# Second MoE's input weights scaled per item and made while they are narrowed, next block's differences spread over steps, and the tail's maxima in three steps

## The chip, the cores and the metric

One Trainium2 chip, one core of it. The metric is the device time of one execution in microseconds, median of several runs. TensorE (PE) multiplies, VectorE (DVE), ScalarE (ACT) and GpSimd (POOL) do the elementwise work, SyncE (SP) issues nearly all transfers.

## The reference, cut to what matters

```python
# q, k, v: (4, 8, 576, 64); rotary embedding on q and k, softmax attention, then
x = attn_out.transpose(0, 2, 1, 3).reshape(2304, 512)
h = np.maximum(np.maximum(x @ w1, x @ w2), x @ w3)      # 512 x 768 each
y = h @ w_out1                                          # 768 x 512
h = y @ w_in                                            # moe2_w_in: 512 x 2048
g = h * (1.0 / (1.0 + np.exp(-h)))
out = g @ w_out                                         # moe2_w_out: 2048 x 512
```

The weights arrive as 64-bit floats.

## The kernel before, in words

The program has three stages on one core: attention with the first MoE woven in, a tail in which the last batch's first MoE runs alone, and the second MoE.

**Attention.** Four batches of 4 head pairs and 5 query tiles make 80 tile steps (0 to 79), 20 a batch. A step issues its scores on PE (`tile_scores`), their row maximum on DVE (`tile_max`, L453, tile `nb`), two exponentials on ACT (L460), and for older tiles the normalisation (L472), the moves of the probabilities over DMA (`tile_move`, L511, `pt<-e`, four transfers a step on SP's queue), the flip of what they brought on DVE (`tile_flip`, L533) and the products with v (`av`, L578). Between them groups of the first MoE (`group`, L673) are put out by a budget written out by hand (`pace`, `RATE`), so the order of the work on PE is fixed when the program is built; a scheduler that is part of the build may move other engines' instructions within what `issue_after` allows.

**Narrowing.** The 64-bit weights of the second MoE are turned into 32-bit ones by `narrow_w2`, in pieces of 128x256: 32 pieces of `wi` (the input weights), then 32 of `wo`. A piece is loaded (L858), cast on ACT (L229), gets its low bits on DVE in three instructions (L241, L248, L249) and is measured on ACT (L155, a sum of squares into a column of `W.mx`). Each is then stored to DRAM (`zwi`, `zwo`). From step 20 the generator `wprep3` is advanced once a step and once more at every fourth: 1.25 pieces a step. After the 32nd piece the columns are turned into a bound (`root`, three small DVE instructions, L160 to L162, and a reduce, L263), and its maximum over partitions is found: `all_max_a` turns the column on PE (L122) and reduces the row on DVE (L124), `all_max_b` spreads it back over partitions on PE (L130), and `scale_of` makes a power-of-two scale and its inverse in four small DVE instructions (L145 to L148).

**Items.** With `wi`'s one scale known, `prep_w8` makes 16 items, one each 1.7 steps: it loads 128x512 of `zwi` back (`za`), forms four sums or differences of 128x128 blocks on POOL (L971, `zs`), and casts each half to a high (ACT, L948) and a low (DVE, L952) 16-bit part (`w8o`), which go to DRAM (`w8scr`, L979). The second MoE reads them from there.

**The tail.** When attention is done, `for n, _ in enumerate(moe)` runs the last batch's first MoE. At n = 9 `y_split` takes the first block's maximum (L165), turns it, spreads it and casts the block; at n = 15 the same is done for the next (`y7_max`, `y_scales`).

**The second MoE.** The first block goes through `s1`, then four passes J = 0..3, each over two blocks with 8 steps p. `s1_pair` makes 42 products per step with combinations of blocks (a fast product scheme with seven forms); its results are added up on DVE (L1109) and POOL (L1117) and go through a Silu on ACT (L1121). `g_split` makes four sums on POOL (L1050, `gsum`) and casts (L1054, L1055); `second` multiplies with `wo` (L1166). For the next J the block is loaded at p = 0, its maximum taken at p = 1, and at p = 2 `y7_sums` makes its scale and its four differences of 128x512 on POOL (L1138, the list `DIFFS`). The forms follow from p = 3 on.

Of the kernel before, what the change touches and what calls it, by code (L numbers as in the profile page):

```python
# [17 lines left out]
P = 128  # L18
# [4 lines left out]
def fused_kernel(  # L23
# [67 lines left out]
    z_p = right("z_p", 4)  # L91
# [18 lines left out]
    zscr = {nm: dram.tile([P, KC * (F2 // 512) * 512], F32, name="z" + nm) for nm in ("wi", "wo")}  # L110
# [72 lines left out]
    class Weights:  # L183
# [76 lines left out]
        def row_max(self, lo=0, n=None, ma=None):  # L260
            ma = ma or self.maxima(lo, n or self.m)
# [7 lines left out]

        def scale_a(self, n):  # L270
            return all_max_a(self.row_max(0, n))
# [548 lines left out]
    def narrow_w2(W, src, nm):  # L820

        part = {}
        M = W.m * 512 // 256
        for n in range(M + 5):
            if n >= 5:
                W.measure(n - 5)
                if nm == "wi":
                    i, o = divmod(n - 5, 2)  # L830
                    q, c = divmod(i, KC)
                    half, f = divmod(4 * q + 2 * o, HB)
                    nc.sync.dma_start(
                        out=zscr[nm].rearrange("p (f c a i n) -> p f c a i n", c=2, a=2, i=2, n=P)[:, f:f + 2, c % 2, c // 2, half],
                        in_=W.t[n - 5].rearrange("p (f n) -> p f n", n=P),
                    )
                else:
                    nc.sync.dma_start(out=zscr[nm][:, (n - 5) * 256:(n - 4) * 256], in_=W.t[n - 5])
            if 3 <= n <= M + 2:
                with tc.issue_after(last["max"]):  # L840
                    W.narrow_low(part.get(n - 3))
                    W.narrow_b(n - 3, part.pop(n - 3, None))
            if 2 <= n <= M + 1:
                if wide:
                    W.t[n - 2] = z_p.tile([P, 256], F32, tag="z", name="z")
                with tc.issue_after(exps[-1]):
                    W.narrow_a(n - 2, part.get(n - 2), low=False)
            if n < M:
                i, o = divmod(n * 256, 512)
                if nm == "wi":  # L850
                    q, c = divmod(i, KC)
                    from_ = src[c * P:(c + 1) * P, q * 512 + o:q * 512 + o + 256]
                else:
                    from_ = src[i * P:(i + 1) * P, o:o + 256]
                if wide:
                    part[n] = z64_p.tile([P, 256], w1.dtype, tag="z64", name="z64")
                    with tc.issue_after(last["load"]):
                        nc.sync.dma_start(out=part[n], in_=from_)  # L858
                else:
                    W.t[n] = z_p.tile([P, 256], F32, tag="z", name="z")  # L860
                    nc.sync.dma_start(out=W.t[n], in_=from_)
            yield
        t = W.scale_a(n=M)
        yield
        with tc.issue_after(last["score"]):
            W.scale_b("s" + nm, t)
        yield
# [14 lines left out]
    def y_scales(m, w, st):  # L882

        s, i = scale_of(all_max(m), 1, "y")
# [4 lines left out]
        ch = small.tile([P, 1], F32, tag="ch", name="ch")  # L889
        nc.vector.tensor_scalar(out=ch, in0=co, scalar1=2.0 * w, scalar2=None, op0=ALU.mult)  # L890
# [6 lines left out]
    def y_split(r, pool, st):  # L897
        r = flat(r[:, 0:2])
        m = small.tile([P, 1], F32, tag="ym", name="ym")
        absmax(m, r)  # L900
        s, sg, ch, co = y_scales(m, 1, st)
# [21 lines left out]
    SUMS = ((4, 0, 2, ALU.add), (6, 1, 0, ALU.subtract), (5, 4, 1, ALU.subtract), (7, 3, 5, ALU.subtract))  # L923
    DIFFS = ((4, 0, 1), (6, 2, 0), (5, 2, 4), (7, 3, 5))

    HB = NF2 // 2
# [26 lines left out]

    def prep_w8(step):

        sw = half_of(WI, "wi")
        steps = []

        def item(k):
            f, c = divmod(k, 2)  # L960
            z, w = {}, {}

            def load():
                z[0] = za_p.tile([P, 4, P], F32, tag="za", name="za")
                nc.sync.dma_start(out=flat(z[0]), in_=zscr["wi"][:, (2 * f + c) * 512:(2 * f + c + 1) * 512])

            def sums():
                z[4] = zs_p.tile([P, 4, P], F32, tag="zs", name="zs")
                block = lambda i: z[i // 4 * 4][:, i % 4]
                for o, x, y, op in SUMS:  # L970
                    nc.gpsimd.tensor_tensor(out=block(o), in0=block(x), in1=block(y), op=op)  # L971

            def high(a):
                w[a] = w8o_p[0].tile([P, 2, 4, P], F16, tag="w8o", name="w8o")
                cast_high(flat(w[a][:, 0]), flat(z[a]), sw, exps[-1])

            def low(a):
                cast_low(flat(w[a][:, 1]), flat(w[a][:, 0]), flat(z[a]), sw, last["max"])
                nc.sync.dma_start(out=w8scr[:, f, c, :, a:a + 4], in_=w[a])  # L979

# [465 lines left out]
```

## Time and profile before

| | |
|---|---|
| median of 3 runs | 968.85 us (968.54 to 969.66) |
| profiled execution, whole | 970.68 us |
| its span, first to last instruction | 969.0 us |
| granted clock, mean | 0.983 |
| PE busy | 901.6 us (93%) |
| DVE, ACT, POOL busy | 709.6, 609.4, 441.1 us |
| moved by DMA | 146.29 MB |

Busy time is what the profiler records of an engine's own instructions. Matmuls are pipelined, so a busy PE can still be slower than its best. Attention ends near 550 us, the tail near 624 us.

### The profile page before, as it was taken

To read this page: it belongs to the slowest core of one execution; us is meant where nothing else is said; L and a number is where in the kernel's file an instruction comes from. 1 tells how busy PE (TensorE), PEld (TensorE's weight loads), DVE (VectorE), ACT (ScalarE), POOL (GpSimd) and SP (SyncE) were. 2 spreads that over 40 slices of the span, in tenths; PEclk is the share of its full clock that TensorE was granted. 3 is DMA by queue.
4 is the path that set the end of the run, shared out by engine and by line. 5 is a ranking of instruction groups with operands and counts; after the bars stand their busy time and mean duration, and the time that the engine had idled before them with its cause. 6 is when DMAs were issued, how large, how long until landed. Compare 5 with 4: busy or idle time off the path is not lost.

```text
span 969.0 us, 19018 instructions
## 1 busy us (share of the span) xinstructions
PE 901.6 (93%) x6802; PEld 669.0 (69%) x6802; DVE 709.6 (73%) x1271; ACT 609.4 (63%) x1405; POOL 441.1 (46%) x482
## 2 busy tenths in 40 slices
PE   3887998999999999989998999999998999999997
PEld 1443665666665666656654687788887888888886
DVE  6779888877788676898887677465786766856654
ACT  1987677757788777789877534363654545545442
POOL 6745485870325502321211047264486467464363
PEclk9799998999999999999999999999999999999999
DMA  6953035858888985899999763273543434424101
GB/s 154 285 146 108 14 100 126 186 110 179 200 172 196 221 159 135 218 241 228 263 223 204 183 206 110 63 230 113 157 158 99 136 122 136 127 87 137 61 1 44
DMA packets 178798, 146.29 MB, mean 151 GB/s; under 512 B 50960, under 2 KB 160272, under 8 KB 178704
## 3 DMA queue, kind: packets, MB, share of 16 engines
q1 hardware_dynamic: 177200, 144.36, 58.0%
q8 instruction: 54, 0.88, 0.4%
q10 hardware_dynamic: 1504, 0.72, 0.3%
q14 instruction: 40, 0.33, 0.1%
HBM read 90.51 MB, written 26.21 MB: 120 GB/s over the span
## 4 chain that ended last, share of the span: by engine, by line
PE 54%; DMA 8%; DVE 8%; ACT 5%; POOL 4%; issue 3%; SPq 3%; DVEq 0%; ACTq 0%; POOLq 0%
PE m L673 12%; PE m L1103 7%; DMA pt<-e 5%; PE mb L1103 5%; PE c L1166 4%; PE b L1166 4%; PE a L1166 3%; PE xp L578 3%; PE s L443 3%; PE mg L673 3%; POOL gsum L1050 2%; PE d L1166 2%; SPq L511 2%; DVE pt L533 1%; DVE nb L453 1%
## 5 line engine op out<-in xcount | busy, mean ns | idle before, releaser
L673 PEld LDWEIGHTS <-w 128*128 128x128 f16 x1632 | 159.1, 98 | 61.0 <-issue 17.8
L673 PE MATMUL m<-x,w 128*128 128x256 f16 (+1 forms) x1356 | 186.9, 286 | 10.6 <-DVE t L692 5.4
L1166 PEld LDWEIGHTS <-g 128*128 128x128 f16 x1485 | 145.8, 98 | 17.2
L1103 PEld LDWEIGHTS <-w8s 128*128 128x128 f16 x1344 | 131.2, 98 | 16.3 <-issue 1.0
L453 DVE TENSOR_REDUCE nb<-s 128x2 f32<-128x1152 f32 (+1 forms) x80 | 98.6, 1233 | 40.7 <-PE s L443 34.1
L460 ACT ACTIVATE e<-s,nb 128x576 f32<-128x576 f32 x144 | 105.3, 736 | 29.8 <-DVE nb L453 27.2
L472 ACT ACTIVATE e<-e,rec 128x576 f32<-128x576 f32 x144 | 104.1, 767 | 9.3 <-DVE rec L470 8.9
L366 POOL TENSOR_TENSOR w<-qk,sin_sb 128x512 f32<-128x512 f32 (+2 forms) x40 | 43.4, 1087 | 128.1 <-DMA qk<-in_q_dram 122.5
L443 PE MATMUL s<-T 64*128 64x512 f32 x256 | 80.7, 701 | 0.0
L578 PE MATMUL xp<-pt,vd 128*64 128x256 f32 (+1 forms) x512 | 76.5, 414 | 0.2 <-DVE pt L533 0.2
L533 DVE STREAM_TRANSPOSE pt<-pt 128x1024 f32<-128x1024 f32 (+1 forms) x60 | 67.7, 1129 | 11.9 <-DMA pt<-e 11.6
L971 POOL TENSOR_TENSOR zs<-za 128x128 f32<-128x128 f32 x32 | 17.1, 554 | 119.9 <-DVE w8o L952 46.1
L1117 POOL TENSOR_TENSOR z<-t 128x256 f32<-128x256 f32 x32 | 27.1, 847 | 89.0 <-DVE t L1109 53.9
L1055 DVE SCALAR_TENSOR_TENSOR g<-gsum,sg,g 128x1024 f16<-128x1024 f32 x36 | 49.2, 1372 | 24.5 <-ACT g L1054 24.1
L1054 ACT ACTIVATE g<-gsum,sg 128x1024 f16<-128x1024 f32 x36 | 40.9, 1143 | 37.8 <-POOL gsum L1050 37.8
L673 PE MATMUL m<-h,wo 128*128 128x256 f16 (+1 forms) x448 | 61.7, 286 | 0.0
L673 PEld LDWEIGHTS <-wo 128*128 128x128 f16 x512 | 49.7, 98 | 14.7 <-issue 2.0
L578 PEld LDWEIGHTS xp<-pt,vd 128*64 128x64 f32 x512 | 35.1, 136 | 34.4 <-issue 12.3
L944 POOL TENSOR_TENSOR z<-z 128x256 f32<-128x256 f32 x32 | 30.1, 964 | 42.1 <-DMA z<-zwo 41.6
L1166 PE MATMUL b<-w,g 128*128 128x256 f16 x376 | 48.5, 273 | 0.0
L1166 PE MATMUL c<-w,g 128*128 128x256 f16 x376 | 48.1, 274 | 0.0
L1166 PE MATMUL a<-w,g 128*128 128x256 f16 x376 | 47.9, 273 | 0.0
(266 smaller groups left out, 1998.1 us busy)
## 6 DMA issues: line engine op xcount, KB each, us to landing
w8s<-w8scr SPq DMA_DIRECT2D x64, 448.0 KB, 4.3
pt<-e SPq DMA_DIRECT2D x192, 128.0 KB, 4.1
z<-in_moe_w_in_dram SPq DMA_DIRECT2D x32, 256.0 KB, 3.6
z<-in_moe_w_out_dram SPq DMA_DIRECT2D x32, 256.0 KB, 3.9
w8scr<-w8o SPq DMA_DIRECT2D x32, 256.0 KB, 3.6
w<-in_moe_w_dram SPq DMA_DIRECT2D x6, 768.0 KB, 5.0
wo<-in_moe_w_dram SPq DMA_DIRECT2D x6, 768.0 KB, 5.4
qk<-in_q_dram SPq DMA_DIRECT2D x32, 128.0 KB, 3.6
```

Of the source, the lines that this page charges most:

```text
L366: tt(out=w4, in0=t4, in1=sin2, op=ALU.mult)
L443: last["s"] = last["score"] = nc.tensor.matmul(s[:, o:o + 512], qs[r], kt[r], start=True, stop=True).ins
L453: x = nc.vector.tensor_reduce(out=nb[:, 0:m], in_=both(s, 0, 960, 576) if m > 1 else s[:, 0:576], op=ALU.max, axis=AX.X, negate=True)
L460: x = nc.scalar.activation(out=e[:, HK[g]], in_=s[:, SK[g]], func=AF.Exp, bias=nb[:, g:g + 1], accum_out=sm[:, g:g + 1])
L472: nc.scalar.activation(out=e[:, HK[g]], in_=e[:, HK[g]], func=AF.Copy, scale=r[:, g:g + 1])
L533: nc.vector.transpose(out=x, in_=x)
L578: nc.tensor.matmul(xp[r, 0:n], v4[:, g, c, :], turned(c, g), start=False, stop=(c == 3))
L673: x = nc.tensor.matmul(ps[:, 0:n], l, r, start=(first and i == 0), stop=(not more and i == len(passes) - 1))
L1054: nc.scalar.activation(out=h, in_=x, func=AF.Copy, scale=sg_t[jb])
L1055: nc.vector.scalar_tensor_tensor(out=l, in0=x, scalar=sg_t[jb], in1=h, op0=ALU.mult, op1=ALU.subtract)
L1103: nc.tensor.matmul(o, l, r, start=(i == 0), stop=(i == len(passes) - 1))
L1166: x = nc.tensor.matmul(ps, l, r, start=first, stop=last_, skip_group_check=True)
```

## The change

- `narrow_w2` handles `wi` and `wo` in one run of 70 iterations. A piece is placed straight into a half of a `za` tile (two pieces are one item's four blocks); the ring `za` grows from 2 to 4 tiles, the ring `z` goes. The pieces of `wi` are loaded in the items' order, as two rows of 1 KB per partition and not one of 2 KB.
- Each pair of items (f = 0..7) has a scale of its own, from its four pieces: taken, turned and spread in three iterations (`scale_m`, `scale_a`, `scale_b`). Items are then made at once: sums in iterations 4f + 8 and 4f + 9, highs from 4f + 9 to 4f + 12, lows from 4f + 10 to 4f + 13. `zwi` and its loads and stores go, `prep_w8` goes.
- `wi`'s overall scale and `wo`'s are still found, each in three iterations. `wo`'s narrowed pieces are stored two at a time.
- `ch` becomes a tile of 8 columns, one for each f, and the Silu in `s1` is split in two halves, each with its own column.
- The four differences of the next J are issued one a step, at p = 1 to 4.
- In the tail the maximum is taken at n = 8, turned at n = 9, spread at n = 10 (and 15, 16, 17 for the next block), the PE part behind the last group.

```diff
-            if hasattr(WI, "s"):
-                wprep4 = wprep4 or prep_w8(1.7)
-                next(wprep4, None)
+            za_p.bufs = 4
             for _ in range(1 + (j % 4 == 0) if j > 20 else 0):
                 next(wprep3, None)
...
+    def wi_scale(f, m):
+        e = rare.tile([P, 1], F32, tag="wie", name="wie")
+        ei, hi, ii = e.bitcast(I32), half_wi.bitcast(I32)[:, f:f + 1], inv_wi.bitcast(I32)[:, f:f + 1]
+        nc.vector.tensor_scalar(out=e, in0=m, scalar1=2.0 ** -45, scalar2=None, op0=ALU.max)
+        nc.vector.tensor_scalar(out=ei, in0=ei, scalar1=EXPMASK, scalar2=None, op0=ALU.bitwise_and)
+        nc.vector.tensor_scalar(out=hi, in0=ei, scalar1=-1, scalar2=266 << 23, op0=ALU.mult, op1=ALU.add)
+        nc.vector.tensor_scalar(out=ii, in0=ei, scalar1=13 << 23, scalar2=None, op0=ALU.subtract)
+
+    def narrow_w2(WI, WO):
...
+        def load(n):
+            W, i = which(n)
+            if W is WI:
+                k, a = divmod(i, 2)
+                f, c = divmod(k, 2)
+                from_ = wi2[(2 * a + c) * P:(2 * a + c + 1) * P, :].rearrange("p (i f n) -> p f i n", i=2, n=P)[:, f]
...
+        def sums(k):
+            zs[k] = zs_p.tile([P, 4, P], F32, tag="zs", name="zs")
+            block = lambda i: (z, zs)[i // 4][k][:, i % 4]
+            for o, x, y, op in SUMS:
+                nc.gpsimd.tensor_tensor(out=block(o), in0=block(x), in1=block(y), op=op)
...
+        def low(k, a):
+            t = w.pop((k, a))
+            f, c = divmod(k, 2)
+            cast_low(flat(t[:, 1]), flat(t[:, 0]), flat((z, zs)[a][k]), half_wi[:, f:f + 1], last["max"])
+            nc.sync.dma_start(out=w8scr[:, f, c, :, 4 * a:4 * a + 4], in_=t)
+
+        def scale_m(f):
+            m = ma[f] = rare.tile([P, 1], F32, tag="wim", name="wim")
+            nc.vector.tensor_reduce(out=m, in_=WI.maxima(4 * f, 4), op=ALU.max, axis=AX.X)
+
+        def scale_a(f):
+            with tc.issue_after(last["score"]):
+                ma[f] = all_max_a(ma[f])
+
+        def scale_b(f):
+            with tc.issue_after(last["score"]):
+                m = all_max_b(ma.pop(f))
+            wi_scale(f, m)
...
+        for n in range(2 * M + 6):
+            for f in range(HB):
+                if 7 <= n - 4 * f <= 9:
+                    (scale_m, scale_a, scale_b)[n - 4 * f - 7](f)
+            scale_all(n, WI, M + 5, "swi")
+            scale_all(n, WO, 2 * M + 3, "swo")
...
-        ch = small.tile([P, 1], F32, tag="ch", name="ch")
-        nc.vector.tensor_scalar(out=ch, in0=co, scalar1=2.0 * w, scalar2=None, op0=ALU.mult)
+        ch = small.tile([P, HB], F32, tag="ch", name="ch")
+        nc.vector.tensor_scalar(out=ch, in0=inv_wi, scalar1=i, scalar2=2.0 * w, op0=ALU.mult, op1=ALU.mult)
...
-                nc.scalar.activation(
-                    out=g[:, 2 * half:2 * half + 2].rearrange("p t (i n) -> p i t n", i=2),
-                    in_=ps.rearrange("p (i t n) -> p i t n", i=2, t=2), func=AF.Silu, scale=ch,
-                )
+                for e in range(2):
+                    nc.scalar.activation(
+                        out=g[:, 2 * half:2 * half + 2, e * P:e * P + P],
+                        in_=ps[:, e * 256:e * 256 + 256].rearrange("p (t n) -> p t n", t=2), func=AF.Silu, scale=ch[:, 2 * u + e:2 * u + e + 1],
+                    )
...
+        def y7_diffs(J, r, diffs):
             with tc.issue_after(last["gsum"]) if J else nullcontext():
-                for o, x, y in DIFFS:
+                for o, x, y in diffs:
                     nc.gpsimd.tensor_tensor(out=y7_block(r, o), in0=y7_block(r, x), in1=y7_block(r, y), op=ALU.subtract)
...
                 if p == 1 and more:
                     m = y7_max(raw)
+                    raw = y7_place(J + 1, raw)
+                if 0 < p < 5 and more:
+                    y7_diffs(J + 1, raw, DIFFS[p - 1:p])
...
-        if n == 9:
-            st["y0"] = y_split(y0, yt_p, st)
+        with tc.issue_after(last["group"]):
+            if n in (9, 16):
+                top = all_max_a(top)
+            if n in (10, 17):
+                top = all_max_b(top)
+        if n == 8:
+            top = small.tile([P, 1], F32, tag="ym", name="ym")
+            absmax(top, flat(y0[:, 0:2]))
+        if n == 10:
+            st["y0"] = y_split(y0, top, yt_p, st)
...
         if n == 15:
-            st["y7s"] = y_scales(y7_max(st["y7"]), 2, st)
+            top = y7_max(st["y7"])
+        if n == 17:
+            st["y7s"] = y_scales(top, 2, st, True)
```

## Rows read from the trace of the kernel before

**Rows 1.** Page, busy us of each engine, share of the span, instructions.

```profile
PE 901.6 (93%) x6802; PEld 669.0 (69%) x6802; DVE 709.6 (73%) x1271; ACT 609.4 (63%) x1405; POOL 441.1 (46%) x482
```

**Rows 2.** Busy time by stretch: stretch and its length, then each engine, clock, DMA.

```profile
192.00:230.00 38.00, 36.67 (x249) 23.74 (x248) 30.41 (x50) 24.81 (x71) 19.51 (x20) 1.00 0.68 142
230.00:385.00 155.00, 150.71 (x1018) 97.14 (x1017) 117.27 (x230) 117.07 (x332) 44.47 (x47) 1.00 0.83 177
385.00:545.00 160.00, 148.53 (x990) 94.18 (x989) 134.48 (x266) 132.36 (x366) 35.05 (x63) 1.00 0.95 227
583.00:675.00 92.00, 92.00 (x783) 76.39 (x783) 52.64 (x74) 44.89 (x67) 45.34 (x47) 1.00 0.41 131
732.00:750.00 18.00, 15.26 (x123) 12.49 (x122) 10.33 (x26) 8.05 (x12) 10.84 (x10) 0.91 0.36 109
```

**Rows 3.** DVE timeline: the maxima that open steps 30 and 55.

```profile
230.15 0.76 DVE L453 TENSOR_REDUCE nb<-s 128x1 f32<-128x576 f32 x1 [0.76 <-PE s L434]
...
384.93 1.36 DVE L453 TENSOR_REDUCE nb<-s 128x2 f32<-128x1152 f32 x1 [1.89 <-PE s L443]
```

**Rows 4.** Tile z by stretch: DVE, ACT and POOL busy with its instructions.

```profile
230.00:385.00 155.00, 28.60 (x72) 22.11 (x72) 0.00 (x0) 1.00 0.83 177
385.00:545.00 160.00, 32.74 (x93) 28.09 (x92) 0.00 (x0) 1.00 0.95 227
```

**Rows 5.** Tile w8o by stretch: DVE and ACT busy with its instructions.

```profile
230.00:385.00 155.00, 0.75 (x1) 1.33 (x2) 1.00 0.83 177
385.00:545.00 160.00, 24.87 (x31) 21.05 (x30) 1.00 0.95 227
```

**Rows 6.** Groups of DVE instructions, 150 to 560 us: busy us, mean ns.

```profile
L124 DVE TENSOR_REDUCE amax<-tr 1x1 f32<-1x128 f32 x4 | 1.1, 274 | 0.0
...
L160 DVE TENSOR_SCALAR wi2m<-wi2m 128x32 f32<-128x32 f32 x1 | 0.2, 171 | 0.0
...
L263 DVE TENSOR_REDUCE wm<-wi2m 128x1 f32<-128x32 f32 x1 | 0.2, 165 | 0.0
...
L146 DVE TENSOR_SCALAR swie<-swie 128x1 int32<-128x1 int32 x1 | 0.2, 154 | 0.0
```

**Rows 7.** Busy time by stretch, shorter ones, as in the second group.

```profile
400.00:425.00 25.00, 22.68 (x158) 14.88 (x158) 23.45 (x48) 21.38 (x64) 3.75 (x8) 1.00 0.93 243
385.00:418.00 33.00, 31.40 (x207) 19.97 (x206) 29.12 (x55) 25.42 (x72) 12.78 (x19) 1.00 0.87 231
418.00:451.00 33.00, 29.84 (x217) 20.16 (x215) 28.11 (x62) 31.29 (x90) 5.85 (x12) 1.00 1.01 233
354.00:385.00 31.00, 31.00 (x204) 19.50 (x203) 20.18 (x39) 21.09 (x55) 3.22 (x3) 1.00 0.54 105
150.00:175.00 25.00, 22.66 (x130) 13.73 (x130) 20.33 (x40) 18.48 (x49) 11.91 (x14) 0.86 0.56 119
```

**Rows 8.** Waits of DVE, 375 to 550 us: total us, times, longest.

```profile
DVE pt L533 <- DMA pt<-e: 11.6, 6, 3.5
```

**Rows 9.** DMA issues: count, KB each, median us to landing.

```profile
zwi<-z SPq DMA_DIRECT2D x32, 128.0 KB, 3.4
za<-zwi SPq DMA_DIRECT2D x16, 256.0 KB, 4.1
```

**Rows 10.** PE timeline, 545 to 583 us: the turns and spreads of maxima.

```profile
547.60 0.27 PE L122 MATMUL tr<-ident,wm 128*1 128x128 f32 x1 [0.61 <-DVE wm L263]
...
575.46 0.38 PE L130 MATMUL m<-amax,ones 1*128 1x1 f32 x2 [1.27 <-DVE amax L124]
...
582.75 0.38 PE L130 MATMUL m<-amax,ones 1*128 1x1 f32 x2 [0.38 <-DVE amax L124]
```

**Rows 11.** Timeline of POOL, DVE and PE around 740 us, in that order.

```profile
730.87 3.71 POOL L1138 TENSOR_TENSOR ye<-x 128x512 f32<-128x512 f32 x2
734.54 1.26 POOL L1138 TENSOR_TENSOR ye<-x,ye 128x512 f32<-128x512 f32 x1
735.76 0.72 POOL L1117 TENSOR_TENSOR z<-t 128x256 f32<-128x256 f32 x1
...
738.10 1.80 DVE L1055 SCALAR_TENSOR_TENSOR g<-z,sg,g 128x768 f16<-128x768 f32 x1 [3.99 <-ACT g L1054]
...
742.84 0.27 PE L122 MATMUL m<-ident,ym 128*1 128x128 f32 x1 [2.65 <-DVE t L1109]
```

More of the change, by code (lines that the diff above doesn't have):

```diff
@@ L109, in fused_kernel @@
     w8scr = dram.tile([P, NF2 // 2, 2, 2, 8, P], F16, name="w8scr")
-    zscr = {nm: dram.tile([P, KC * (F2 // 512) * 512], F32, name="z" + nm) for nm in ("wi", "wo")}
+    zscr = {nm: dram.tile([P, KC * (F2 // 512) * 512], F32, name="z" + nm) for nm in ("wo",)}
     ps_am, b_now = [], [0]
@@ L818, in fused_kernel @@
     NQ = F2 // 512
[L820 to L835, printed above, removed]
-                    )
-                else:
-                    nc.sync.dma_start(out=zscr[nm][:, (n - 5) * 256:(n - 4) * 256], in_=W.t[n - 5])
-            if 3 <= n <= M + 2:
+    HB = NF2 // 2
@@ new lines, in fused_kernel @@
+    SUMS = ((4, 0, 2, ALU.add), (6, 1, 0, ALU.subtract), (5, 4, 1, ALU.subtract), (7, 3, 5, ALU.subtract))
+    half_wi = const.tile([P, HB], F32, name="half_wi")
+    inv_wi = const.tile([P, HB], F32, name="inv_wi")
+    def wi_scale(f, m):
[5 more added lines that the diff above has]
+        nc.vector.tensor_scalar(out=ii, in0=ei, scalar1=13 << 23, scalar2=None, op0=ALU.subtract)
@@ L840, in narrow_w2 @@
                 with tc.issue_after(last["max"]):
                     W.narrow_low(part.get(n - 3))
-                    W.narrow_b(n - 3, part.pop(n - 3, None))
-            if 2 <= n <= M + 1:
+                    W.narrow_b(i, part.pop(n - 3, None))
+            for f in range(HB):
+                k, s = 2 * f, n - 4 * f
+                for at_, g, q, h in ((9, high, k, 0), (10, high, k + 1, 0), (11, high, k, 1), (12, high, k + 1, 1)):
+                    if s == at_:
+                        g(q, h)
+                if s in (8, 9):
+                    sums(k + s - 8)
@@ L844, in narrow_w2 @@
+            if 2 <= n <= 2 * M + 1:
+                W, i = which(n - 2)
                 if wide:
-                    W.t[n - 2] = z_p.tile([P, 256], F32, tag="z", name="z")
+                    place(n - 2)
                 with tc.issue_after(exps[-1]):
[L847 to L861, printed above, removed]
@@ L862, in narrow_w2 @@
-            yield
[L863 to L867, printed above, removed]
+                    W.narrow_a(i, part.get(n - 2), low=False)
+            if 3 <= n <= 2 * M + 2:
+                W, i = which(n - 3)
+                W.measure(i)
+            if n >= M + 4 and n % 2 and n <= 2 * M + 3:
+                i = n - 4 - M
+                nc.sync.dma_start(out=zscr["wo"][:, (i - 1) * 256:(i + 1) * 256], in_=flat(z.pop((n - 4) // 2)))
@@ L880, in y_load, with y_scales @@
         return t
-    def y_scales(m, w, st):
-        s, i = scale_of(all_max(m), 1, "y")
+    def y_scales(m, w, st, behind=False):
+        if not behind:
+            m = all_max(m)
+        s, i = scale_of(m, 1, "y")
         sg = small.tile([P, 1], F32, tag="sg", name="sg")
@@ L895, in y_scales, with y_split @@
         return s, sg, ch, co
-    def y_split(r, pool, st):
+    def y_split(r, m, pool, st):
         r = flat(r[:, 0:2])
-        m = small.tile([P, 1], F32, tag="ym", name="ym")
-        absmax(m, r)
-        s, sg, ch, co = y_scales(m, 1, st)
+        s, sg, ch, co = y_scales(m, 1, st, True)
         yt = pool.tile([P, 2, KC, 256], F16, tag="yt", name="yt")
@@ L952, in cast_low @@
             nc.vector.scalar_tensor_tensor(out=l, in0=x, scalar=s, in1=h, op0=ALU.mult, op1=ALU.subtract)
[L954 to L979, printed above, removed]
-            t = k * step
-            for d, fn in ((0, load), (2, sums), (2.1, lambda: high(0)), (2.9, lambda: low(0)), (3, lambda: high(4)), (3.9, lambda: low(4))):
-                steps.append((t + d, fn))
-        for k in range(2 * HB):
-            item(k)
-        yield from timed(steps)
     def prep_w7(stage, w7_p, w7, step):
@@ L1120, in s1_pair @@
                 x = g[:, :, e * P:e * P + P]
-                nc.scalar.activation(out=x, in_=x, func=AF.Silu, scale=ch)
+                nc.scalar.activation(out=x, in_=x, func=AF.Silu, scale=ch[:, p:p + 1])
             if e:
@@ L1324, in fused_kernel @@
     WO = st["wo"] = Weights(None, "wo2", NF2, DM, 512 // 256)
[L1326 to L1330 removed]
+    wprep3 = narrow_w2(WI, WO)
     for j, _ in enumerate(attention(), 1):
@@ L1355, in fused_kernel @@
     for _ in wprep3:
-        pass
-    for _ in wprep4:
         pass
```

59 lines of the change are left out of this document (45 added, 14 removed).

## Prediction

> **What bounds the kernel now.** I read the page's busy times first: PE 901.6 of 969.0 us [rows 1], so time can come only from where PE stands still or runs at half its clock. Busy time by stretch shows where [rows 2]. From 583 to 675 us PE is busy 92.00 of 92 us; nothing is to be had there. From 732 to 750 it is idle 2.74 of 18 us, with the clock at 0.91. In attention it is idle 4.29 us of 230 to 385 and 11.47 us of 385 to 545. The maxima at 230.15 and 384.93 us open tile steps 30 and 55 [rows 3], so these stretches are steps 30 to 54, in which `wi` is narrowed, and steps 55 to 79, in which `wo` is narrowed and the items are made (the w8o rows are there: 24.87 us on DVE, against 0.75 before [rows 5]). DVE is busy 117.27 of 155 us (76%) in the first and 134.48 of 160 (84%) in the second. The shorter windows show what a loaded DVE does [rows 7]: at 20.18 of 31 us PE never stops; at 29.12 of 33 (88%) PE idles 1.6 us; at 23.45 of 25 (94%), the fullest window, 2.3 us. DVE's share is the number on which the change turns.
>
> **The items move from the second stretch to the first.** Iteration n of the new run comes at about step 20 + n/1.25. Lows come one an iteration from n = 10 to 41, steps 28 to 53; everything that made items in the second stretch now lies in the first, beside `wi`'s narrowing and POOL's rotary work.
>
> DVE in steps 30 to 54, from its present 117.27 us [rows 2]: the present narrowing goes (28.60 [rows 4]) and so does the stray low (0.75 [rows 5]). Back come 25 steps at 1.25 pieces, 31.25 pieces. One piece is 61.34 us over 55 pieces (72 + 93 instructions, three a piece [rows 4]), 1.115 us, so 34.8. Then 29 lows at 24.87/31 = 0.80 us [rows 5]: 23.2. Then seven scales. One is nine small instructions: three for the root at 0.17, a reduce of 0.165, the row's reduce of 0.274, four like the 0.154 one [rows 6], about 1.55 us; seven are 10.9. Together 156.8 us in a stretch that lasts 155.
>
> So DVE becomes the bound of these 25 steps. How full it can get is the unknown. Full to the last nanosecond they take 156.8 (+2). At the highest share seen, 0.94 [rows 7], 166.8 (+12). At the 0.88 of the highest step-long window they take 178 (+23). I take 0.94, since a queue that always has work behind it should reach what a mixed one reached for 25 us. ACT gets fuller too: 117.07 - 22.11 - 1.33 + 31.25 pieces at 0.92 + 29 highs at 0.70 [rows 2, 4, 5] is 143 of 155 us (92%), which speaks against the low end. In steps 20 to 29 the first lows and two scales, some 5 us, go on a DVE that is busy 30.41 of 38 [rows 2]: 93%, under the share I allow, so nothing.
>
> PE gets eight more turns and spreads at 0.27 and 0.38 us [rows 10], 5.2 us. They are covered by PE's waiting for DVE in the same steps; with DVE at its full share that cover is gone and up to 5 us come on top. What is queued behind: a spread stands on PE after the last scores, and the groups and the next scores stand behind it; its sum waits for DVE's row reduce.
>
> DVE in steps 55 to 79: 134.48 less narrowing 32.74 and lows 24.87, plus 22 pieces at 1.115 and one scale: 103 of 160 us, 64%. That is the share of the window 354 to 385, in which PE never stops [rows 7]. DVE's 11.6 us of waiting for the moves `pt<-e`, all between 375 and 550 us [rows 8], should shrink with SP's queue: there the 16 loads of `za` go and half of the `zwo` stores. PE's 11.47 us of idle time can fall to nothing (-11.5) or to the first stretch's present rate, 4.29 of 155 (-7). I take the middle, -9.
>
> The traffic itself, 32 stores of 128 KB and 16 loads of 256 KB [rows 9], I price at nothing: no chain of the trace ends on these transfers, and in the first stretch the stores to `w8scr` take the place of those to `zwi`. Rows of 1 KB instead of 2 KB in `wi`'s loads: nothing, since loads run some iterations ahead; bound from above by the landing of 4.1 us once, at the start [rows 9].
>
> **The tail.** PE waits 0.61 us for the column's reduce, 1.27 and 0.38 us for two row reduces [rows 10]. Three steps with a whole group between put 1 to 2 us of other matmuls in each gap, and `wo`'s scale now falls inside attention (iterations 67 to 69, near step 75). All 2.3 us go; at worst none.
>
> **The differences.** At 730.87 us POOL runs two differences in 3.71 us and a third in 1.26, ahead of L1117's sum at 735.76. ACT's Silu and casts queue behind that sum, DVE's L1055 waits 3.99 us for them, and the PSUM bank that PE needs for turning the maximum comes free late: PE waits 2.65 us [rows 11]. Soon after the granted clock falls to 1.2 GHz: 0.91 over 18 us is 1.6 us more [rows 2]. With one difference a step, the third and fourth move to p = 3 and 4 and the first to p = 1. L1117 comes 1.26 to 3.1 us earlier; the 2.65 us wait ends with the upper figure and is halved by the lower. I take all of it: 2.74 + 1.6 = -4.4; bounds 0 and -4.4. Blocks that never stalled have nothing to gain.
>
> **Costed at nothing.** The halved Silu in `s1`: PE is full from 583 to 675 while ACT has 44.89 of 92 us [rows 2]; doubling all of ACT's work would still fit. `ch` with eight columns replaces one small instruction by one.
>
> **Sum.** +12 - 9 - 2.3 - 4.4 = -3.7 on the profiled 970.7, so 967.0. That execution is 1.8 us above the median of 968.85, so I forecast 965.1 for the median, 965.
>
> **Rivals.**
> 1. *DVE does not get fuller than 0.88.* Then the first 25 steps cost 23: +23 - 9 - 2.3 - 4.4 = +7, 976. For it: the full windows of a whole step group stop at 0.88, ACT is at 92% in the same steps, and each waits for the other (maximum, exponential, reciprocal). Against it: 23.45 of 25 us was reached [rows 7]. It decides from 156.8/x = 155 + 15.7: below a share of 0.92 the change gains nothing.
> 2. *The first stretch takes it all.* DVE runs full and the second stretch loses all its idle time: +2 - 11.5 - 2.3 - 4.4 = -16, 952. For it: PE's own work stays the same and PE idles only 4.29 us there now.
> 3. *The stall at 742 us stays,* because the scheduler lets the first differences crowd in as before: -3.7 + 4.4, about 969.5, no change.
> 4. *The clock falls in the first stretch.* After the stalls near 157 us the granted clock is 0.86 over 25 us, 1.2 GHz for part of it: 3.5 us lost [rows 7]. Two such falls where PE waits for DVE add 7: 972. Against it: the clock is 1.00 through 385 to 545 with 11.47 us of idle time in small pieces [rows 2]. The Trainium skill ("TensorE: Matmul & The Clock Gate", What's actually happening) says that the throttled state is the default and that activity lifts it; by that rule a PE made to wait for DVE pays twice, and the trace agrees only where the waits are long, as at 742 us.
>
> **How the numbers follow.** Forecast 0.37, rivals in order 0.24, 0.20, 0.13, 0.06. A measurement of this kernel can tell about 0.2%, 1.9 us, from no change. Faster: the second rival and nearly all of the forecast's case, 0.54. Same: the third and a little of the forecast's, 0.16. Slower: the first and fourth, 0.30. The forecast's own range is 960 to 969. For 8 in 10 I go down to 953, which leaves out half of the second rival, and up to 976, which leaves out less than half of the first: 953 to 976.
>
> **What would show it.** Right: DVE above 90% busy in steps 30 to 54, those steps longer by 8 to 16 us, steps 55 to 79 shorter by 7 to 11; no L122 or L130 wait over 0.5 us after 545 us; no drop of the clock near 740. Wrong: steps 30 to 54 longer by over 16 us, or not longer at all (then small instructions and lows cost less than their rows, or the iterations come later than I count); a new wait of ACT for lows when the ring `za` is full.

## The result: slower by 1.4%

The changed kernel took 981.99 us (median of 6 runs, 978.77 to 984.72) against 968.52 us (6 runs, 966.80 to 969.66): a ratio of 1.0138, 95% interval 1.0113 to 1.0164 (below, each time has the ratio to the kernel before that ran beside it, with this interval in brackets). The forecast was 965, the range 953 to 976. The profiled execution took 979.21 us, near the low end of its runs, and its span is 977.5 us.

Busy times on the page of the changed kernel, to lay beside [rows 1]:

```profile
PE 910.2 (93%) x6826; PEld 669.8 (69%) x6826; DVE 725.4 (74%) x1339; ACT 612.0 (63%) x1413; POOL 448.4 (46%) x482
```

The next two views give busy time by stretch, columns as in [rows 2], cut where the maxima open steps 30, 35, 45, 55 and 75 and where the second MoE's matmuls begin. The kernel before, in the order steps 30 to 54, of these 35 to 44, steps 55 to 74, from step 75 to the second MoE, and the second MoE:

```profile
230.20:384.90 154.70, 150.41 (x1015) 96.89 (x1013) 117.15 (x229) 116.87 (x332) 44.37 (x47) 1.00 0.83 177
259.60:323.70 64.10, 59.81 (x406) 38.56 (x407) 54.16 (x109) 50.46 (x150) 32.86 (x37) 1.00 0.85 185
384.90:514.50 129.60, 119.84 (x808) 77.02 (x809) 109.92 (x215) 106.75 (x299) 31.21 (x55) 1.00 0.94 233
514.50:623.90 109.40, 105.26 (x795) 76.51 (x794) 73.34 (x142) 56.20 (x121) 34.05 (x40) 1.00 0.56 147
623.90:968.90 345.00, 336.51 (x3058) 299.61 (x3056) 225.96 (x373) 168.57 (x257) 189.65 (x201) 0.99 0.38 117
```

The changed kernel, the same five stretches:

```profile
227.50:403.60 176.10, 162.70 (x1047) 101.90 (x1046) 157.68 (x338) 137.96 (x380) 73.69 (x94) 0.98 0.84 194
257.50:339.70 82.20, 72.42 (x475) 46.61 (x474) 78.09 (x158) 60.37 (x166) 51.36 (x60) 0.96 0.80 184
403.60:525.00 121.40, 119.35 (x803) 76.65 (x803) 92.20 (x194) 94.01 (x275) 7.81 (x8) 1.00 0.79 167
525.00:632.30 107.30, 105.65 (x789) 76.83 (x790) 64.10 (x110) 47.94 (x97) 30.83 (x32) 1.00 0.42 110
632.30:977.40 345.10, 336.03 (x3059) 298.34 (x3056) 228.99 (x373) 170.77 (x265) 189.61 (x201) 1.00 0.37 117
```

Read the second column against the other view: +21.4 in steps 30 to 54 (forecast +12), -8.2 and then -2.1 behind them (-9 and -2.3), and nothing in the second MoE (-4.4). The prediction's own sign of being wrong has come: steps 30 to 54 are longer by over 16 us. And DVE is busy 0.895 of them (157.68 of 176.10), not above 0.90. DVE's demand in steps 30 to 54 is 157.68 us, as summed (156.8), but half of it lies in steps 35 to 44, where DVE is busy 78.09 of 82.20 us. It waits for next to nothing there, and PE stands idle 9.8 us. Over the whole kernel PE's idle time has not grown (67.3 us against 67.4): nearly all of the 8.5 us by which the span grew is recorded as PE busy (910.2 against 901.6). Some instructions there are also longer than the rows they were priced by. DVE, then POOL, in the order of time, changed kernel:

```profile
283.95 1.33 DVE L247 TENSOR_SCALAR za<-za 128x256 int32<-128x256 int32 x1
285.21 0.15 DVE L825 TENSOR_SCALAR wie<-tr 128x1 f32<-128x1 f32 x1
285.27 1.49 DVE L695 TENSOR_TENSOR h<-t,h 128x256 f16<-128x256 f32 x1
...
292.44 1.24 DVE L160 TENSOR_SCALAR wi2m<-wi2m 128x4 int32<-128x4 int32 x1
```

```profile
283.71 1.42 POOL L362 TENSOR_TENSOR w<-qk,sin_sb 128x512 f32<-128x512 f32 x1 [2.84 <-DMA qk<-in_q_dram]
285.21 1.27 POOL L363 TENSOR_TENSOR qk<-qk,cos_sb 128x512 f32<-128x512 f32 x1
...
291.86 1.80 POOL L366 TENSOR_TENSOR qk<-qk,w 128x512 f32<-128x512 f32 x1
```

L160 works on four columns and takes 1.24 us. It ends at 293.68 us, POOL's L366 at 293.66. It is the longest of its kind: the median of the eight L160 on four columns in this kernel is 0.172 us. The Trainium skill ("SBUF — State Buffer", Who interferes with whom) says that a DVE instruction in a mode that uses two ports contends with GpSimd, that whichever issues first has the shared pair of ports for its whole instruction and the other is blocked, and that `tensor_scalar` can enter such a mode; the trace agrees, with L160 starting 0.58 us behind L366 and ending with it.

From step 20 on the profiled executions account for 10.1 us of the 13.5 (822.0 us to the end against 811.9). The rest is not placed: executions of the changed kernel lie 6 us apart, and the profiled one is among the shortest of them, while that of the kernel before (970.68 us) is longer than all six of its runs here.

### The profile page after: what moved, and what is told of

Read it like the earlier page. It is cut to its first block, busy times and chain, and to the rows that moved or that the text cites. A ratio compares the mean times of both kernels' runs of the same rounds, so it can differ in the third digit from the quotient of the medians.

```text
span 977.5 us, 19039 instructions
## 1 busy us (share of the span) xinstructions
PE 910.2 (93%) x6826; PEld 669.8 (69%) x6826; DVE 725.4 (74%) x1339; ACT 612.0 (63%) x1413; POOL 448.4 (46%) x482
## 4 chain that ended last, share of the span: by engine, by line
PE 47%; DVE 7%; ACT 3%; DMA 3%; POOL 3%; issue 2%; SPq 1%; DVEq 0%; ACTq 0%; POOLq 0%
PE m L669 9%; PE m L1137 6%; PE mb L1137 5%; PE xp L574 3%; PE c L1204 3%; PE b L1204 3%; PE a L1204 3%; PE mg L669 3%; PE s L439 2%; POOL gsum L1083 2%; DVE g L1088 2%; PE d L1204 2%; DMA pt<-e 1%; PE mb L1104 1%; PE m L1104 1%
## 5 line engine op out<-in xcount | busy, mean ns | idle before, releaser
L1204 PEld LDWEIGHTS <-g 128*128 128x128 f16 x1485 | 145.2, 98 | 17.7 <-DVE t L1215 0.9
L449 DVE TENSOR_REDUCE nb<-s 128x2 f32<-128x1152 f32 (+1 forms) x80 | 98.6, 1232 | 47.6 <-PE s L439 38.5
L456 ACT ACTIVATE e<-s,nb 128x576 f32<-128x576 f32 x144 | 105.3, 736 | 28.6 <-DVE nb L449 25.8
L574 PE MATMUL xp<-pt,vd 128*64 128x256 f32 (+1 forms) x512 | 80.4, 418 | 0.4 <-DVE pt L529 0.4
L529 DVE STREAM_TRANSPOSE pt<-pt 128x1024 f32<-128x1024 f32 (+1 forms) x60 | 67.6, 1127 | 5.1 <-DMA pt<-e 5.1
L1087 ACT ACTIVATE g<-gsum,sg 128x1024 f16<-128x1024 f32 x36 | 40.8, 1141 | 30.9 <-POOL gsum L1083 30.6
L363 POOL TENSOR_TENSOR qk<-qk,cos_sb 128x512 f32<-128x512 f32 (+2 forms) x44 | 48.7, 1109 | 2.5
```

The source lines that it names most:

```text
L363: tt(out=t4, in0=t4, in1=cos2, op=ALU.mult)
L449: x = nc.vector.tensor_reduce(out=nb[:, 0:m], in_=both(s, 0, 960, 576) if m > 1 else s[:, 0:576], op=ALU.max, axis=AX.X, negate=True)
L456: x = nc.scalar.activation(out=e[:, HK[g]], in_=s[:, SK[g]], func=AF.Exp, bias=nb[:, g:g + 1], accum_out=sm[:, g:g + 1])
L529: nc.vector.transpose(out=x, in_=x)
L574: nc.tensor.matmul(xp[r, 0:n], v4[:, g, c, :], turned(c, g), start=False, stop=(c == 3))
L1204: x = nc.tensor.matmul(ps, l, r, start=first, stop=last_, skip_group_check=True)
```

## The experiments

Theory A: the loss is DVE's work in the crowded steps 35 to 44. Theory B: the new turns and spreads of the seven scales hold PE up there. The first four kernels are edits of the changed kernel (kernel before, beside them: 969.21 us). The edits are cut to the lines that matter; `...` marks what is left out.

**The iterations spread.**

```diff
-            for _ in range(1 + (j % 4 == 0) if j > 20 else 0):
+            rate = 0 if j <= 20 else 1 + (j % 4 == 0) if j < 34 else int(j % 2 == 0) if j < 48 else 1 + (j % 2 == 0)
+            for _ in range(rate):
```

> The changed kernel with another pace of the narrowing: 1.25 iterations a step up to step 33, one every second step in steps 34 to 47, 1.5 a step after. No work is left out. Theory A (in steps 35 to 44 VectorE has no time left, 78 us of work in 82 us, and the time follows its work there): about 7 pieces, 7 lows and 2 scales leave the crowded steps, some 15 us of VectorE's time, so 967 to 973 us against 982. Theory B (the eight new turns and spreads of maxima stall TensorE by their round trips, whatever VectorE's load): their number is the same, 979 to 983.

977.63 us, ratio 1.0094 (1.0063 to 1.0125). Steps 35 to 44 take 64.5 us, as in the kernel before: the loss there follows the iterations away. Most of it comes back where they went, in steps 50 to 64:

```profile
355.60:391.40 35.80, 34.76 (x224) 21.17 (x223) 31.89 (x80) 28.78 (x81) 8.27 (x16) 1.00 0.79 188
391.40:428.10 36.70, 32.91 (x226) 22.31 (x226) 33.41 (x78) 28.56 (x77) 14.35 (x17) 0.95 0.85 207
428.10:465.20 37.10, 34.68 (x223) 21.38 (x220) 26.83 (x64) 29.05 (x89) 0.00 (x0) 0.91 0.78 180
```

These are five steps each; such a block took 30.9 to 33.1 us before. Some 5 us of it is the clock (0.95 and 0.91 in the last two blocks).

**One scale for all items** (leaves out seven scales: 7 turns, 7 spreads, 63 small DVE instructions; every item uses the first pair's scale). There are eight scales, one for each pair of items, though the title says per item.

```diff
...
-                if 7 <= n - 4 * f <= 9:
+                if f == 0 and 7 <= n <= 9:
...
```

> The changed kernel with the scale of the first item pair used for all eight; the scales of the other seven pairs are left out (7 turns and spreads on TensorE, 63 small VectorE instructions). Theory A: only VectorE's time of these counts, 11 us by their rows and some of it outside the crowded steps, so 971 to 977 us. Theory B: nearly all of the 13.5 us goes, 967 to 971.

978.41 us, 1.0102 (1.0067 to 1.0138): most of the loss stays without the turns, and steps 30 to 54 take 172.3 us. That is above the range of either theory. Theory B falls as the main cause, since it wanted nearly all of the 13.5 us back and got 3.6.

**Low bits of `wi` left out** (its float64 halves lose their low bits).

```diff
-                    W.narrow_low(part.get(n - 3))
+                    if W is WO:
+                        W.narrow_low(part.get(n - 3))
```

> The changed kernel without the instruction that makes the low bits of the input weights' pieces (32 VectorE instructions of 0.47 to 0.55 us; the last bits of these weights are left as they come). Theory A: some 10 us of VectorE's work leave steps 30 to 47 and the time falls by 7 to 12 us, 970 to 975. Theory B: the turns and spreads are untouched, 979 to 983.

977.97 us, 1.0090 (1.0055 to 1.0124).

**The same low bits on ACT** (nothing left out): the edit above, and

```diff
-                    W.narrow_a(i, part.get(n - 2), low=False)
+                    W.narrow_a(i, part.get(n - 2), low=W is WI)
```

> As the run without the low bits, but ScalarE makes them, 32 instructions of about 0.45 us; no work is left out. Theory A with ScalarE having room (30 of 41 us busy in steps 35 to 39): 971 to 976 us. If ScalarE is as tight as VectorE, 977 to 983. Theory B: 979 to 983.

977.63 us, 1.0091 (1.0060 to 1.0122). In both, steps 35 to 44 take 76 to 77 us instead of 82.2: the direction of theory A, but none of the four kernels came down into theory A's range, and the time is still far above 969, though DVE's busy time in the whole of the last one, 710.9 us, is within 1.3 us of the kernel before.

Kernel before, beside the next four: 968.84 us.

**The differences alone**, on the kernel before.

```diff
...
                 if p == 1 and more:
                     m = y7_max(raw)
+                    raw = y7_place(J + 1, raw)
+                if 0 < p < 5 and more:
+                    y7_diffs(J + 1, raw, DIFFS[p - 1:p])
```

> The kernel before with the differences alone placed one in a step (y7_place, y7_diffs), nothing else changed. By the prediction's term D the wait of 2.65 us near 742 us and the fall of the clock behind it go: -4.4 us, about 964.5, ratio 0.9955. By the rival (the wait is shared out over the step's end and other steps, as the trace of after suggests: POOL is busy back to back from 705 to 745 us with or without the move) the second MoE keeps its 309.5 us from the first s1_pair's stage to the end, and the time stays within 1.5 us of before.

967.87 us, 0.9995 (0.9980 to 1.0011): the rival, no change. PE's waits between 692 and 762 us (total us, times, longest), first in the kernel before, then in this one:

```profile
PE m L122 <- DVE t L1109: 2.6, 1, 2.6
PE m L1103 <- DVE t L1109: 0.4, 1, 0.4
```

```profile
PE m L1103 <- DVE t L1109: 2.0, 3, 1.4
PE b L1170 <- DVE t L1181: 0.6, 1, 0.6
PE mb L1103 <- DVE ga L1109: 0.5, 1, 0.5
PE m L122 <- DVE t L1109: 0.3, 1, 0.3
```

The one wait of 2.65 us [rows 11] has shrunk to 0.3, but the waits of this window add up to 3.4 us, where they were 3.0. The clock stays at 1.00 from 732 to 750 us (0.91 before), and yet the second MoE is as long as before, 345.2 us.

**The tail alone**, on the kernel before: the edits at n = 8, 9, 10 and 15, 16, 17.

> The kernel before with the two maxima of the tail (y0 and y7) alone taken, turned and spread in three steps; wo's scale stays where it was. By the prediction's term C two of the three waits go, 1.27 + 0.38 us: about 967.3, ratio 0.998, and PE's waits for the row reduces in 545 to 583 us fall under 0.2 us each. If a group between the steps doesn't cover them, no change.

967.71 us, 0.9997 (0.9981 to 1.0013). The stretch from step 75 to the second MoE takes 107.9 us against 109.4 in the profiles; PE's waits for the row reduces between 540 and 590 us fall from 1.7 to 0.2 us, as expected. In the time, the expected 1.65 us lies within the interval, and so does nothing.

**The four differences together again**, on the changed kernel.

```diff
-                if 0 < p < 5 and more:
-                    y7_diffs(J + 1, raw, DIFFS[p - 1:p])
                 if p == 2 and more:
                     sums = y7_sums(J + 1, raw, y_scales(m, 2, st))
+                    y7_diffs(J + 1, raw, DIFFS)
```

> The changed kernel with all four differences again at p = 2; all else as changed. If one difference a step is worth the 4.4 us of term D, this is slower than the changed kernel: about 986. If the move is worth nothing, it is the same as the changed kernel, 982 within 2 us, and the second MoE is again 309 to 311 us long. If the move itself costs (new waits at J = 0's end and p = 1), about 978 to 980.

980.64 us, 1.0128 (1.0111 to 1.0145), the changed kernel's time. The old wait is back (L121 for L1143, 2.7 us), and the second MoE takes 345.4 us. (The expectation's 309 to 311 us are counted from a later start than these 345.)

**A pace by what an iteration costs**, with the low bits on ACT.

```diff
+            pace_w = 0 if j <= 20 else 4 if j < 35 else 3 if j < 47 else 5 if j < 61 else 7
+            for _ in range(j * pace_w // 4 - (j - 1) * pace_w // 4):
```

> The changed kernel with the narrowing paced by what an iteration costs DVE: 1 iteration a step to step 34, 3 in 4 steps in the rotary steps 35 to 46, 5 in 4 to step 60, 7 in 4 after it (wo's iterations have no items), and the low bits of wi on ACT as in the run before; nothing is left out. If the loss is one of crowding (the steps' total DVE demand fits, at about 88% of attention's time), the loss of steps 30 to 54 mostly goes without coming back: 965 to 969. If DVE's total is too much wherever it lies, it comes back as in the first spread run: 975 to 979. Steps 35 to 44 should take 64 to 66 us, steps 55 to 64 under 65.

976.63 us, 1.0092 (1.0074 to 1.0109). Steps 35 to 44 take 67.6 us, but steps 55 to 64 take 69.5 (66.2 before). What is lost there is partly the clock, two stretches beside one another:

```profile
407.00:413.00 6.00, 4.15 (x31) 2.62 (x27) 4.75 (x13) 3.25 (x9) 1.94 (x4) 1.00 0.87 230
413.00:421.00 8.00, 6.99 (x28) 3.85 (x29) 6.09 (x11) 6.32 (x20) 2.01 (x4) 0.57 0.64 197
```

PE stood idle 1.85 of 6 us, all of it the first part of one wait of 2.65 us for ACT, and then ran at 1.2 GHz for most of 8 us. The clock fell at 301 and 560 us too.

Kernel before, beside the next four: 967.93 us.

**Items kept off the rotary steps:** the same edit with `4 if j < 35 else 2 if j < 45 else 5 if j < 55 else 2 if j < 62 else 8`.

> The changed kernel with the low bits of wi on ACT, and the narrowing and the items kept off the rotary steps: 1 iteration a step to step 34, 1 in two steps in 35 to 44 and in 55 to 61, 5 in 4 between, 2 a step after 61. If the loss arises where the rotary steps meet the items (DVE full, PE waiting, the granted clock falling behind the wait), no block of five steps is over 35 us, the clock doesn't fall between 230 and 545 us, and the time is 966 to 970. If the load comes back wherever the items lie, as in the two runs with other paces, 975 to 978.

974.90 us, 1.0071 (1.0044 to 1.0098): the best of the paces, and still 7 us slower. The block of steps 40 to 44 takes 38.9 us, with DVE busy only 28.4; the clock falls in it, at 319.6 us.

**Lows left out** (the items' low parts are not made; the high part is stored twice).

```diff
-            cast_low(flat(t[:, 1]), flat(t[:, 0]), flat((z, zs)[a][k]), half_wi[:, f:f + 1], last["max"])
-            nc.sync.dma_start(out=w8scr[:, f, c, :, 4 * a:4 * a + 4], in_=t)
+            nc.sync.dma_start(out=w8scr[:, f, c, :, 4 * a:4 * a + 4], in_=t[:, 0:1].to_broadcast([P, 2, 4, P]))
```

> The changed kernel with the items' 32 low parts left out (the high part is stored twice); all else as changed. Takes some 25 us off DVE's demand in steps 28 to 53 and nothing off PE, POOL or the DMA queues. If DVE's demand sets the length of these steps: steps 35 to 44 at 67 to 70 us (82.2 in the changed kernel), no clock fall there, and 966 to 970 in all. If what is lost there is lost to something else (POOL, PE's extra turns, the loads), over 975.

972.22 us, 1.0042 (1.0026 to 1.0058), a little above the expected figures; steps 35 to 44 take 72.9, and against the expectation the clock falls once in them, at 297 us. Of the 13.5 us lost, 9 go with instructions that run on DVE alone.

**POOL's sums left out** (the second half of an item is made from z again).

> The changed kernel with POOL's four sums of each item left out (the second half of an item is made from z again); DVE and ACT run the same instructions. If POOL's work beside it lengthens DVE's instructions (z L240 550 ns against 512, small ones 355 against 171 ns), DVE's busy time in steps 35 to 44 falls from 78.1 to 71 to 74 us and these steps from 82.2 to 74 to 78. If DVE's instructions are as long without the sums, no change there, and the time is 980 to 983.

980.00 us, 1.0118 (1.0091 to 1.0146). DVE's busy time in steps 35 to 44 falls from 78.09 to 70.9 us though it runs the same instructions, and these steps take 77.2. Part of that has only moved: in steps 20 to 54 DVE's busy time falls by 4.1 us (216.83 to 212.72), in the whole kernel by 1.2 (725.4 to 724.2). POOL does lengthen DVE's work, but by less than the ten steps suggest. The whole gains some 2 us at most, with the clock at 0.91 in these steps; the intervals of the two ratios overlap.

**A bare load on DVE**, on the kernel before (30 reductions that nobody reads).

```diff
...
+        if 35 <= j < 45:
+            for _ in range(3):
+                with tc.issue_after(last["max"]):
+                    nc.vector.tensor_reduce(out=load_t, in_=flat(cos_sb), op=ALU.max, axis=AX.X)
```

> The kernel before with 30 idle reductions of 320 columns on DVE (about 0.4 us each, 12 to 13 us in all, read by nobody), three in each of steps 35 to 44. If DVE's demand sets the length of the steps once it is near full (54.2 of 64.1 us busy now), they take 69 to 73 us and the time is 974 to 978 without any item in them. If DVE still has room there, or the loss needs the items' own waits, 64 to 66 us in these steps and 969 to 970 in all.

974.64 us, 1.0063 (1.0040 to 1.0086). The load, and steps 35 to 44:

```profile
L1347 DVE TENSOR_REDUCE load_t<-cos_sb 128x1 f32<-128x320 f32 x30 | 14.0, 466 | 0.0
```

```profile
259.10:327.40 68.30, 61.86 (x423) 40.77 (x422) 62.55 (x137) 49.61 (x150) 31.73 (x36) 0.98 0.82 187
```

With no item, scale, turn or store added, DVE's work alone makes the kernel slower: 6.7 us for 14.0, or 0.48 us for each us (0.28 to 0.59 by the interval).

That left the question whether only full steps pay. Kernel before, beside the next three: 968.31 us.

**The same load in steps with room**, two reductions in each of steps 30 to 34 and 45 to 54.

> The kernel before with the same 30 idle reductions as in the run before (14.0 us of DVE in all), but two in each of steps 30 to 34 and 45 to 54, where DVE has 63 of 90.6 us, instead of three in each of steps 35 to 44, where it has 54 of 64. If a load costs time only where DVE is near full, these steps stay within 1 us and the time is 968 to 970. If every us of DVE work costs about half a us wherever it lies, 974 to 976.

973.88 us, 1.0062 (1.0046 to 1.0077): 5.6 us for 13.8, or 0.40 (0.32 to 0.54). The loaded blocks rose by 1.0, 0.0 and 2.6 us; another 3.3 came in steps 35 to 44, for which no load was written (DVE 59.21 us against 54.16):

```profile
260.10:327.50 67.40, 61.94 (x406) 39.09 (x404) 59.21 (x112) 50.35 (x150) 39.32 (x40) 0.97 0.85 198
```

DVE ran two of the reductions and the same 39 narrowing instructions there as before, but these took 4.5 us longer, beside one more set of rotary work on POOL (39.32 us against 32.86). So a load does not act only where it is written, and this run doesn't separate place from amount; it does show that room in a block is no cover.

**The other two parts together**, the differences and the tail, on the kernel before.

> The kernel before with the two other parts of the change, the differences one in a step and the tail's two maxima in three steps, and without the moved items. By the prediction's terms C and D 962.5 to 963; by the two runs of the parts alone (ratios 0.9995 and 0.9997) 967.5 to 968.5, no change that can be told.

968.48 us, 1.0006 (0.9994 to 1.0018).

**The same, with narrowing faster outside the rotary steps** (iterations a step: 1.5, then 1 in steps 35 to 44, 1.5 to step 54, 1.25).

> The same, with the narrowing paced faster outside the rotary steps (3 in two steps to step 34 and in 45 to 54, 1 a step in 35 to 44, 5 in 4 after), so that wi is done, and the reloaded items start, some three steps earlier, in steps where DVE has room, and the rotary steps get less. If the place of the DVE work decides, steps 35 to 44 shorten by about 1 us, steps 55 to 79 by 2 to 4, and the time is 963 to 966. If only the total counts, no change against the run beside it.

974.28 us, 1.0069 (1.0046 to 1.0092): wrong in sign. Against the kernel before, steps 30 to 54 gain 0.8 us, steps 55 to 74 lose 6.0 (135.6 against 129.6), though DVE has only 2.9 us more in them (112.77 against 109.92). Items and narrowing that start earlier meet in steps 55 to 64, which now take 70.9 us.

Kernel before, beside the last two: 967.36 us.

**The changed kernel once more.**

> The changed kernel itself once more, nothing edited, since its executions lie 6 us apart and the one profiled was among the shortest. If its loss sits where the first profile showed it: steps 30 to 54 at 173 to 181 us, steps 55 to 74 at 120 to 123, the second MoE at 309 to 311, and the time 979 to 984. If the spread comes from elsewhere, another stretch differs by over 2 us.

981.13 us, 1.0138 (1.0108 to 1.0168). The stretches are 174.4, 121.7, 106.9 and 345.2 us (the last counted from the first product, as above): the loss is where the first profile had it.

**The load in the second stretch**, two reductions in each of steps 60 to 74 of the kernel before.

> The kernel before with the 30 idle reductions (14.0 us of DVE), two in each of steps 60 to 74 of the second stretch, where DVE has 80.7 of 96.5 us. If DVE's work costs 0.4 to 0.5 us for each us wherever it lies, as in steps 35 to 44 and in 30 to 54, 974 to 975, and the -8.2 us of the changed kernel's second stretch is the same rate on the 24 us that DVE lost there. If the second stretch is cheaper because its bound is another (PE waits for moves there), under 971.

975.16 us, 1.0077 (1.0056 to 1.0097): 7.8 us for 13.8, or 0.57 (0.39 to 0.68). The three rates can't be told apart.

## Why the prediction was wrong

**The items' move (+12 forecast, +21.4 measured): the step that failed.** The sum of the work was right, by its parts too: in steps 30 to 54 narrowing took 36.0 us of DVE (forecast 34.8), lows 22.9 (23.2), scales 9.5 (10.9). The price was not. I took 0.94 as the share to which DVE fills; it was 0.895. And I took DVE's work to be free until DVE is full, so that I asked only how full it can get. The bare loads show a price well below that: 0.40 to 0.57 us for each us, with DVE at 0.79 and 0.82 of steps 30 to 54 in the two that lie there. Steps 30 to 54 by the busy view, against 154.70 us long with 117.15 of DVE; the last two columns are told of below the table:

| kernel | DVE more | steps longer | for each us | maxima later | clock |
|---|---|---|---|---|---|
| bare load in steps 35 to 44 | 10.5 | 6.6 | 0.63 | 5.9 | 0.99 |
| bare load elsewhere | 15.0 | 6.9 | 0.46 | 4.3 | 0.99 |
| kept off the rotary steps | 11.6 | 11.9 | 1.03 | 5.1 | 0.98 |
| pace by cost | 15.1 | 9.9 | 0.66 | 6.6 | 0.99 |
| lows left out | 18.3 | 11.1 | 0.61 | 5.2 | 0.99 |
| iterations spread | 18.8 | 8.1 | 0.43 | 11.7 | 1.00 |
| low bits on ACT | 29.1 | 16.9 | 0.58 | 12.4 | 0.98 |
| low bits left out | 32.7 | 16.2 | 0.50 | 12.9 | 0.97 |
| sums left out | 34.5 | 18.0 | 0.52 | 11.2 | 0.96 |
| one scale | 35.3 | 17.6 | 0.50 | 21.6 | 0.99 |
| changed kernel | 40.5 | 21.4 | 0.53 | 21.7 | 0.98 |

At half a us for each, 40 us more would have been forecast as +20. The first rival's 23 us was nearer than my 12, but its reason falls as well: the bare load leaves DVE at 0.79 of the 25 steps, far under 0.88, and costs time.

How DVE's work costs time where it seems to have room can be seen in one step of the changed kernel. PE, DVE and ACT, in that order:

```profile
293.03 1.13 PE L439 MATMUL s<-T 64*128 64x512 f32 x4
...
302.29 0.79 PE L436 MATMUL s<-kd,T 128*128 128x128 f32 x2 [2.21 <-ACT e L456]
```

```profile
294.60 0.74 DVE L1020 SCALAR_TENSOR_TENSOR w8o<-zs,half_wi,w8o 128x512 f16<-128x512 f32 x1
...
297.74 1.00 DVE L248 SCALAR_TENSOR_TENSOR za<-z,za 128x256 int32<-128x256 int32 x2
298.66 1.34 DVE L449 TENSOR_REDUCE nb<-s 128x2 f32<-128x1152 f32 x1
```

```profile
300.69 0.73 ACT L456 ACTIVATE e<-s,nb 128x576 f32<-128x576 f32 x1
```

The scores are done at 294.16 us. Their maximum (L449) starts 4.5 us later, behind a low (L1020), the narrowing (L248) and others in DVE's queue; the exponentials (L456) can't start before it ends at 300.00, and start at 300.69; PE's next scores (L436) wait 2.21 us for them. Summed over steps 30 to 54, the maxima start 29.2 us behind the end of their scores, against 7.5 before: 21.7 us later, beside 21.4 us of length. The column "maxima later" gives this difference for each kernel, "clock" the granted clock of the stretch. It follows the length only roughly, since other waits and the clock take part. In steps 55 to 74 it falls from 14.6 to 4.9 us in the changed kernel, and where narrowing was paced faster it rises to 20.3, with the 6.0 us that DVE's amount alone doesn't explain.

Two things blur the table. The build orders PE's work anew for each kernel, so first-MoE matmuls move as well: 624 of them lie in steps 30 to 54 against 614, 640 with the bare load in steps 35 to 44 and 634 with the iterations spread. At 0.14 us each (58.2 us for 420 of them before) these two rates fall to 0.29, the others to 0.40 to 0.53, and only that of the items kept off the rotary steps stays high (0.92). And part of the loss isn't DVE's total. From step 30 to the second MoE, where such moves cancel, the changed kernel has 13.6 us more DVE work and takes 11.1 us longer; without the lows it has 9.1 us less and takes 0.8 longer, with the low bits on ACT 2.1 more and 6.4 longer. So some 5 of the 11 us stay when DVE's total is nearly that of before. Seen in the trace, but not separated by a run, are the turns and spreads, which the prediction held to be covered (6.2 us of PE in steps 30 to 54 against 1.4), and the clock.

**Evenness.** A step lasts 6 us and DVE's load came in lumps: steps 35 to 44 hold rotary work on POOL and DVE beside the items. Spreading the iterations emptied these steps but filled others, and no pace brought the changed kernel's median under 974.

**The clock (fourth rival) came as well.** Changed kernel, two stretches beside one another, columns as in [rows 2]:

```profile
296.00:302.00 6.00, 2.26 (x19) 1.60 (x17) 6.00 (x11) 4.57 (x15) 2.51 (x6) 0.99 0.47 139
302.00:309.00 7.00, 6.71 (x25) 3.70 (x26) 5.98 (x15) 4.17 (x14) 4.37 (x6) 0.52 0.81 209
```

DVE is busy all 6 us, PE 2.26: it waits 1.82 us for ACT's L407, which is queued behind an instruction that waited 1.34 us for DVE, and 2.21 us for the exponentials shown above. Then PE runs most of 7 us at 1.2 GHz, some 3.4 us lost, within the 21.4. The kernel before has no such fall between 192 and 545 us [rows 2].

**The second stretch (-9 for steps 55 to 79, measured -8.2 by step 74): right.** DVE is at 76%, POOL nearly silent, and PE idle 2.05 of 121.4 us. How much counts as this term hangs on the cut at step 75; with the tail it is -10.3 of the forecast -11.3. It also shows why the change could not pay. In steps 55 to 74 DVE gave up 17.7 us and 8.2 came back, 0.46 for each, close to the first stretch's rate; from step 75 on it gave up 9.2 and 2.1 came back, with PE's idle time down from 4.1 to 1.65 us. So DVE took on 40.5 us and was relieved of 27 (183.26 us from step 55 to the second MoE before, 156.30 after), and the last of these gained little because PE was nearly full.

**The tail (-2.3, measured -2.1 in its stretch): right in the profile,** but alone it is too small to be told from nothing. PE's waits for row reduces behind 545 us are gone. Against the prediction's sign, one L121 still waits 0.9 us there, for the maximum itself (DVE L164).

**The differences (-4.4, measured 0): wrong,** as the third rival had it in amount. The wait of 2.65 us and the clock's fall did go, so that rival's mechanism (the first differences crowd in as before) isn't what happened. In the six profiled kernels with the differences together the clock falls once between 739 and 755 us, in the thirteen with them spread never. POOL's work from 692 to 745 us is nearly the same in sum (41.41 us before, 42.74 with the differences alone), and PE waits at other places instead, for 3.4 us in all against 3.0. That the differences, moved earlier, delay the sums of other steps is argued, not shown. The step that failed is "blocks that never stalled have nothing to gain": they had something to lose.

**No version beat the kernel before.** The change without its moved items (1.0006, 0.9994 to 1.0018) is as fast as it, within 0.2%.

## What to carry to other kernels

Where one engine sits in the dependent chain of every step, don't price added work at nothing because its busy share leaves room: load the kernel with instructions that nobody reads and measure the rate first (0.40 to 0.57 us for each us here), and read from the trace how long that chain's instruction waits in the engine's queue. When work moves from one stretch to another, price both ends separately; the end that is relieved gains only down to the bound of the next engine. Before a stretch's length is read as a loss, count the work that moved into it. When one long wait is taken away by issuing its cause earlier, list whose queue the cause now stands in front of.

## What was not expected of the hardware

A DVE instruction on 128x4 took 1.24 us beside a POOL instruction that read two tensors, against a median of 0.172 us for the eight of its kind in the same kernel. Leaving out 64 POOL instructions took 4.1 us off DVE's own unchanged work in steps 20 to 54, and 1.2 us off it in the whole kernel. And PE was granted half its clock for most of the next 7 us after two waits of 1.82 and 2.21 us, in the run with the pace by cost after one wait of 2.65 us.
